# The two first wqkv loads of a one-core mixer kernel, issued from ScalarE's queue instead of SyncE's

## The chip, the cores and the metric

The kernel runs on one core of one Trainium2 chip. The metric is the device time of one execution in microseconds (us), the median of several executions. Engines are named as in the profile: PE (TensorE matmul), PEld (TensorE weight load), DVE (VectorE), ACT (ScalarE), POOL (GpSimd), SP (SyncE, which computes nothing and issues DMAs). An engine name with q behind it (SPq, PEq) is that engine's instruction sequencer.

## The reference

The input `x` has 2048 rows of 512. All tensors are fp32.

```python
xn = layernorm(x)
s  = A(xn, wqkv, wo)            # dilated sliding-window attention
g  = silu(B(xn, w1, b1, w2, b2))
out = x + s * g

def A(x, wqkv, wo):             # 32 heads of 16, window 8, dilation 2
    q, k, v = split(x @ wqkv)   # wqkv: 512 x 1536
    # each position attends to positions pos, pos-2, ..., pos-14
    return softmax(q k^T / 4, masked) v @ wo

def B(x, w1, b1, w2, b2):       # layernorm -> dense 1376 -> gelu -> dense 512
    return gelu(layernorm(x) @ w1 + b1) @ w2 + b2
```

## The kernel before

The 2048 positions are split into two classes by parity (dilation 2), and each class into 8 row tiles of 128. The 32 heads form 4 head blocks of 8; a pass over one head block makes q, k and v of 8 row tiles with PE (line 912) and then the window's logits and sums on DVE and POOL. The two dense layers of B run between these passes (lines 1192 and 1236), and the output projection is at lines 1104 and 1136. fp32 operands are split into a high and a low fp16 part and multiplied in three products; so weights and activations are scaled, cut and subtracted on ACT, DVE and POOL before PE can use them.

Every operation of the kernel is recorded in a plan with what it reads and writes. The table `ORDER` then says in which order the operations are written into the program: each engine runs its own in that order, and waits are put in where data or buffers need them. No engine passes over one of its instructions that still waits. A DMA is recorded as an operation of a queue `sp`, and is written as `nc.sync.dma_start`, so SP issues it. A DMA is also made to wait for the one that used its completion semaphore before it; there are eight such semaphores in turn.

What matters here is the start of the program. SP issues the loads; up to the ninth their order is

- **x0**, row tile 0 of x (256 KB, line 1283),
- **T7** and **T6**, the transposed row tiles 7 and 6 (256 KB each, line 1308),
- **x1**, row tile 1 (256 KB),
- **Q0**, first half of head block 0 of wqkv (384 KB, line 593, 128 partitions of 3072 bytes),
- **x2**, row tile 2 (256 KB),
- **Q2**, the second half of that block (384 KB, line 593),
- more tiles of x (256 KB each), then the next head block and the weights of B (line 1310).

Q0 and Q2 land in the two halves of a buffer `prod`. They are used twice. ACT squares each half and sums the squares (line 602, `scale_q`); PE adds the sums over partitions (line 518), DVE makes a scale of it (lines 529 to 547), and ACT and others cut the scaled weights into high and low parts (lines 632, 639, 558). And PE multiplies the raw fp32 halves with T7 and T6, whose mean has been taken off (line 724, `direct`: results `z` for T7 and `pl` for T6; the first two of the four steps over k read Q0, the other two Q2).

Before these stands, on PE, a row of matmuls on constants (line 1355), the means of T7 and T6 (lines 701 and 713), and the transposes of the normalised row tile 0 (line 808). That tile's path is: x0 lands, DVE takes its statistics (lines 672, 673, 753), POOL the root (757) and the normalisation (787), then PE transposes, ACT copies the result (812). For row tile 1 the normalisation is on ACT (783); its statistics are taken together with those of row tile 2, so it needs x2 too.

Of the kernel before, what the change touches and what calls it, by code (L numbers as in the profile page):

```python
# [13 lines left out]
ALU = mybir.AluOpType  # L14
# [4 lines left out]
P = 128  # L19
# [12 lines left out]
NFB = 7  # L32
LASTC = (0, 256, 512)
LASTPOOL = (0, 2, 4)
NX = 5

W1C = [0, 2048, 4096, 5120, KT * F]
# [30 lines left out]
MEANBY = ('dve', 'pe', 'pool', 'pool')  # L68
W2LATE = 6
SUBS = ()  # L70
ST_ENG = ('dve',) * 8
YLO = ('dve',) * 8
SECS = BATCHES
# [334 lines left out]
def tile_mixer(ctx, tc, a_x, a_xt, a_xo, a_wqkv, a_wo, b_w1, b_b1, b_w2, b_b2, out):  # L408
    nc = tc.nc
# [14 lines left out]
    def pe(n, cols, fn, r, w, fp32=1, **k):  # L424
        pl.add("pe", n * cols * 0.423e-3 * fp32, fn, r, w, **k)

    def dve(n, fn, r, w, f=1.0, port=True, c=0.065, **k):
        pl.add("dve", c + n * DVE1 * f, fn, r, w, port=port, **k)
# [4 lines left out]
    def pool(dur, fn, r, w, port=True, **k):  # L433
        pl.add("pool", dur, fn, r, w, port=port, **k)

    def dma(nbytes, fn, r, w, **k):
        pl.add("sp", 0.0, fn, r, w, nbytes=nbytes, **k)
# [52 lines left out]
    def f32v(t, k):  # L490

        names = " ".join("abcdefg"[:len(t.shape) - 1])
        return t.rearrange(f"p {names} -> p ({names})").bitcast(F32).rearrange(
            "p (k f) -> p k f", k=k)
# [67 lines left out]
    def split(hi, lo, src, s, r, w, eng="act", n=None, low="dve"):  # L562
# [8 lines left out]
        if low == "pool":  # L571
# [9 lines left out]
    stq = [lambda: xq0.t[:, 0:1536], lambda: U[1][:, 2048:3584],  # L581
           lambda: f32v(yT[2], 1)[:, 0, 0:1536], lambda: f32v(yT[3], 1)[:, 0, 0:1536]]
# [3 lines left out]
    def k0(hb):  # L586
        return dict(rate=400e3, tail=0.6, issue=0.45) if hb == 0 else dict(tail=3.5) if hb > 1 else {}


    def load_q(hb, kk=range(0, KT, 2)):  # L590
        pre = pl.users([x for x in stkey[hb] if x is not xq0])
        for k in kk:
            dma(P * 3072, lambda k=k: nc.sync.dma_start(stq[hb]()[:, k * 384:(k + 2) * 384],
                                                        a_wqkv[hb, :, k * 384:(k + 2) * 384]),
                [], [("stq", hb, k), ("stq", hb, k + 1)] + stkey[hb], after=pre, **k0(hb))

    def scale_q(hb):
# [88 lines left out]
    def parts(i):  # L686
        return ((0, 1), (1, KT)) if i in SUBS else ((0, KT),)

# [43 lines left out]
    def stats_act(i):  # L732
        q, (x, xkey) = cpos[i], xk[i]
        sm = R_s.new()
        o, dst = (i % 4) * P, yT[i // 4]
        junk = dst[:, 0, :, o:o + P].bitcast(BF16)
        act(512, lambda: nc.scalar.activation(x(), x(), AF.Identity, accum_out=sm.t[:, 0:1]), [xkey], [xkey, (sm, 0)], aps=2)
        act(1, lambda: nc.scalar.activation(mv0[:, q, 0:1], sm.t[:, 0:1], AF.Identity, scale=1.0 / D), [(sm, 0)], [("mv0", i)])
        act(1, lambda: nc.scalar.activation(sm.t[:, 1:2], sm.t[:, 0:1], AF.Identity, scale=-D ** -1.5), [(sm, 0)], [(sm, 1)])
        act(512, lambda: nc.scalar.activation(  # L740
            junk, x().rearrange("p (k t) -> p k t", k=KT), AF.Square, bias=sm.t[:, 1:2], scale=D ** -0.5,
            accum_out=mv0[:, q, 1:2]), [xkey, (sm, 1), ("mv0", i)], [("mv0", i), ("yh", 0, i)], aps=3)

    def ln0(g):
        q, n = cpos[g[0]], len(g)
        for i in g:
            if ST_ENG[i] == "act":
                stats_act(i)
# [377 lines left out]
    def wo_last():  # L1126
        rings = [R_ps, R_ps, R_ps, R_pl] + R_z
        end = PR_M * 10
        early, late = range(NHB - 1), [NHB - 1]
        rw = [("oT", hb, h) for hb in early for h in range(2)] + [("wo", k) for k in (0, 2)]  # L1130

        def mm(b, i, hbs, cols, start, stop):
            def go():
                for hb in hbs:
                    for n, (s, t) in enumerate(((0, 0), (0, 1), (1, 0))):
                        nc.tensor.matmul(b.t[:, cols], wo[:, t, hb, i % 4 * P:(i % 4 + 1) * P],  # L1136
                                         oT[:, hb, i // 4, s].rearrange("p t x -> p (t x)")[:, cols],
                                         start=(start and hb == 0 and n == 0), stop=(stop and hb == NHB - 1 and n == 2))
            return go

        parts = [(i, slice(0, D)) for i in range(NI - 1)] + [(NI - 1, slice(a, b)) for a, b in zip(LASTC, LASTC[1:])]
        banks = {}
        for n, (i, cols) in enumerate(parts[:NI]):
            b = banks[n] = rings[n].new()
            w = cols.stop - cols.start
            pe(9, w, mm(b, i, early, cols, True, False), rw + [("A", 7)] * (rings[n] is R_pl), [b], prio=end + 2 * n)
        for i in range(4):
            dma(P * 2048, lambda i=i: nc.sync.dma_start(gu[i], gd[1, i]),
                [("gd", 1, i), ("U0end",)], [("gu", i)], prio=end)
        xs = {}  # L1150
        for n, (i, cols) in enumerate(parts):
            w = cols.stop - cols.start
            if n < NI:
                if i < 7:
                    xb = R_f.new()
                    xs[i] = (lambda xb=xb: xb.t), xb
                else:
                    xs[i] = (lambda: U[0][:, NI * D:(NI + 1) * D]), ("gux",)
                dma(P * 2048, lambda x=xs[i][0], i=i: nc.sync.dma_start(x(), xo[1, i]),
                    [("oT", NHB - 2, 0), ("U0end",)], [xs[i][1]], prio=end + i)  # L1160
                b = banks[n]
                pe(3, w, mm(b, i, late, cols, False, True), [("oT", hb, i // 4) for hb in late], [b], prio=end + 2 * n + 1)
            else:
                b = R_ps.new()
                pe(12, w, mm(b, i, range(NHB), cols, True, True), rw + [("oT", hb, i // 4) for hb in late], [b],
                   prio=end + 2 * n + 1)
            x, xkey = xs[i]
            g = gu[i][:, cols]
            dve(w, lambda b=b, g=g, cols=cols: nc.vector.scalar_tensor_tensor(  # L1169
                g, b.t[:, cols], osc[:, 2:3], g, op0=ALU.mult, op1=ALU.mult),  # L1170
                [b, ("gu", i), ("osc",)], [("gw", n)], port=False, c=0.125)
            if n in LASTPOOL:
                pool(1.27, lambda x=x, g=g, cols=cols: nc.gpsimd.tensor_tensor(g, g, x()[:, cols], op=ALU.add),
                     [("gw", n), xkey], [("gw", n)])
            else:
                dve(w, lambda x=x, g=g, cols=cols: nc.vector.tensor_tensor(g, g, x()[:, cols], op=ALU.add),  # L1176
                    [("gw", n), xkey], [("gw", n)])
            dma(P * 4 * w, lambda g=g, i=i, cols=cols: nc.sync.dma_start(ov[1, i][:, cols], g),
                [("gw", n)], [("out", 1, n)], tail=0.7)
# [119 lines left out]
    s2a, s2b = f32v(yT[2], 4), f32v(yT[3], 4)  # L1299
    s2c = [R_f.new() for k in range(NX)]  # L1300

    def load(kind, i, last=()):
        if kind == "q":
            load_q(i // 4, [i % 4])
        elif kind == "x":
            load_x(i, 1)
        elif kind == "t":
            dma(P * 2048, lambda: nc.sync.dma_start(xt[i], a_xt[FP.index(i)]), [], [("xt", i)], rate=395e3, tail=0.6, issue=0.45)
        elif kind == "w":
            dma(P * 4 * (W1C[i + 1] - W1C[i]), lambda: nc.sync.dma_start(  # L1310
                s1[i](), b_w1[:, W1C[i]:W1C[i + 1]] if i < 3 else b_w1[:, W1C[3]:].rearrange("p (k e) -> p k e", k=KT)), [], s1k[i],
                rate=400e3, tail=0.8)
        elif kind == "s":
            dma(P * 8192, lambda: nc.sync.dma_start((s2a, s2b)[i], b_w2[:, 4 * i:4 * i + 4]), last,
                [("yT", 2 + i), ("s2", i)])
        elif kind == "b":
            dma(P * 428, lambda: nc.sync.dma_start(b1T, b_b1), [], [("b1T",)], rate=60e3)
        else:
            p0, w = (FL, D) if i == 4 else (0, D if i < 3 else P)
            dma((P - p0) * 4 * w, lambda: nc.sync.dma_start(s2c[i].t[p0:P, 0:w], b_w2[p0:P, 8 + i, 0:w]), last, [s2c[i]])  # L1320
# [32 lines left out]
    for n in range(WAKE):  # L1353
        b = R_z[0].new()
# [18 lines left out]
    with pl.fuse():  # L1373
# [14 lines left out]
                                           op1=ALU.max), [ssh], [ssh], port=False)  # L1388
# [4 lines left out]
    for m, (f0, f1) in enumerate(W1P):  # L1393
        n = min(f0 // 4, 2) if f0 < 10 else 3
# [32 lines left out]
    for m, k in enumerate(W2P):  # L1427
        n, K = (2, P) if k < 8 else (1, P)
# [32 lines left out]

    pl.prio = PR_U + 800
    load_q(2)
    prep_q(2)
    pl.prio = PR_U + 900
    load_q(3)
    prep_q(3)

# [16 lines left out]
    osc = sb.tile([P, 4], F32, name="osc")  # L1485
# [89 lines left out]
```

## Time and profile before

| | us |
|---|---|
| median of 3 executions (406.83, 406.97, 408.04) | 406.97 |
| the profiled execution | 407.78 |
| its span, first to last instruction | 406.0 |
| PE busy in it | 399.9 |
| DVE busy | 377.6 |
| ACT busy | 237.8 |
| POOL busy | 133.0 |

The profiled execution's own time is 1.78 us over its span. Busy time is summed over instructions and a busy PE need not be at its peak, so PE's 399.9 us say that it hardly ever stands idle, and not more. DMA queues: one queue (q1, issued by SP) carries all data, 47.82 MB.

### The profile page before, as it was taken

The numbers are of one execution on the slowest core, as the hardware profiler recorded it, in microseconds if no ns is written. First come the engines' busy times: TensorE is split into PE (matmuls) and PEld (weight loads), VectorE is DVE, ScalarE is ACT, GpSimd is POOL, SyncE is SP. The second block draws the span as 40 slices with busy tenths as digits, with TensorE's granted clock in tenths as the row PEclk, the third lists the DMA queues.
The fourth block names the chain that finished last, engine by engine and source line by source line (L and its number), as shares of the span: only waits on it lengthen the run. The fifth ranks groups of instructions, "written<-read, shape, count | busy, mean of one in ns | idle before, by whom it ended". The sixth has DMA issues, their size and how long they took to land.

```text
span 406.0 us, 5527 instructions
## 1 busy us (share of the span) xinstructions
PE 399.9 (99%) x2030; PEld 199.3 (49%) x2030; DVE 377.6 (93%) x382; ACT 237.8 (59%) x408; POOL 133.0 (33%) x139
## 2 busy tenths in 40 slices
PE   7999999999999999999999999999999999999996
PEld 5665544444444455445544554444455544444443
DVE  5998999999998999999999989999899889999966
ACT  2999889789689545775383243215252567345260
POOL 4713000072562534242524424242524204250012
PEclk9999999999999999999999999999999999999999
DMA  7948826240039260804571016231430755205566
GB/s 273 412 104 212 255 73 174 84 160 2 1 68 226 71 105 0 192 11 106 109 193 53 0 31 172 94 102 31 148 105 0 137 123 146 82 27 136 136 157 233
DMA packets 53827, 48.17 MB, mean 119 GB/s; under 512 B 38236, under 2 KB 38808, under 8 KB 53288
## 3 DMA queue, kind: packets, MB, share of 16 engines
q1 hardware_dynamic: 53800, 47.82, 43.7%
q8 instruction: 16, 0.26, 0.3%
q14 instruction: 11, 0.09, 0.1%
HBM read 24.27 MB, written 7.34 MB: 78 GB/s over the span
## 4 chain that ended last, share of the span: by engine, by line
PE 96%; DMA 2%; SPq 1%; DVE 1%; ACT 0%; issue 0%; DVEq 0%
PE ps L912 30%; PE ps L1192 26%; PE z L1236 26%; PE ps L1104 5%; PE z L1136 2%; PE ps L1136 2%; PE z L1224 2%; DMA prod<-in_A_wqkv_dram 2%; PE pl L912 1%; PE pl L1136 1%; PE pl L724 1%; PE z L808 0%; PE z L1227 0%; SPq L1283 0%; DVE U L1169 0%; DVE U L1176 0%
## 5 line engine op out<-in xcount | busy, mean ns | idle before, releaser
L912 PE MATMUL ps<-wq,yT 128*128 128x384 f16 (+1 forms) x708 | 129.5, 337 | 0.0
L1236 PE MATMUL z<-h,w 128*128 128x512 f16 x480 | 112.2, 379 | 0.0
L1192 PE MATMUL ps<-yT,w 128*128 128x512 f16 x480 | 108.9, 379 | 0.0
L912 PEld LDWEIGHTS <-yT 128*128 128x128 f16 x744 | 72.4, 98 | 58.4 <-issue 0.5
L1192 PEld LDWEIGHTS <-w 128*128 128x128 f16 x480 | 46.7, 98 | 55.7 <-issue 0.5
L978 DVE TENSOR_TENSOR prod<-U 128x2048 f32<-128x2048 f32 x32 | 73.2, 2288 | 0.9
L981 DVE TENSOR_REDUCE L<-prod 128x128 f32<-128x2048 f32 x32 | 73.0, 2282 | 0.4
L1236 PEld LDWEIGHTS <-w 128*128 128x128 f16 x480 | 46.7, 98 | 54.0
L1047 POOL TENSOR_TENSOR prod<-prod,prod 128x1024 f32<-128x1024 f32 x14 | 41.4, 2974 | 72.1 <-DVE prod L1036 72.1
L1036 DVE TENSOR_TENSOR prod<-pl,U 128x2048 f32<-128x2048 f32 x28 | 63.4, 2282 | 0.2
L930 ACT ACTIVATE U<-ps,cs 128x384 f32<-128x384 f32 x56 | 31.5, 576 | 48.0 <-PE ps L912 47.4
L1205 ACT ACTIVATE ps<-ps,b1T,hsc 128x512 f32<-128x512 f32 x40 | 29.7, 747 | 36.8 <-PE ps L1192 36.7
L1208 ACT ACTIVATE h<-ps,hsc 128x512 f16<-128x512 f32 x40 | 27.2, 683 | 17.8 <-PE z L1236 9.0
L1057 POOL COPY gate<-prod 1x1 f32<-1x1 f32 x21 | 5.0, 237 | 96.5 <-DVE prod L978 96.5
L1058 POOL TENSOR_TENSOR prod<-prod 128x1024 f32<-128x1024 f32 x14 | 32.9, 2349 | 0.0
L1210 DVE SCALAR_TENSOR_TENSOR h<-ps,hsc,h 128x512 f16<-128x512 f32 x40 | 29.7, 743 | 1.7 <-ACT h L1208 1.7
L1104 PE MATMUL ps<-oT,wo 128*128 128x512 f16 x96 | 22.0, 379 | 0.0
L1019 ACT ACTIVATE o<-prod,osc 128x1024 f16<-128x1024 f32 (+1 forms) x9 | 9.4, 1050 | 20.9 <-POOL prod L1058 10.5
L1205 ACT ACT_TABLE_LOAD x11 | 14.1, 1283 | 11.7 <-PE ps L1192 11.5
L1031 DVE TENSOR_TENSOR prod<-prod,prod 128x2048 f32<-128x2048 f32 x9 | 20.6, 2283 | 0.1
L1058 POOL TENSOR_TENSOR prod<-prod,prod 128x1024 f32<-128x1024 f32 x7 | 16.4, 2344 | 0.0
L992 POOL MEMSET L<- 1x56 f32 (+5 forms) x48 | 4.1, 185 | 37.5 <-DVE L L981 37.5
(194 smaller groups left out, 407.2 us busy)
## 6 DMA issues: line engine op xcount, KB each, us to landing
U<-U SPq DMA_DIRECT2D x16, 392.0 KB, 4.9
f<-in_A_x_dram SPq DMA_DIRECT2D x16, 256.0 KB, 3.0
f<-in_A_xo_dram SPq DMA_DIRECT2D x15, 256.0 KB, 3.8
gd<-f SPq DMA_DIRECT2D x12, 256.0 KB, 2.4
prod<-in_A_x_dram SPq DMA_DIRECT2D x8, 256.0 KB, 6.4
oT<-in_B_w_dram SPq DMA_DIRECT2D x2, 1024.0 KB, 7.8
yT<-in_B_w_dram SPq DMA_DIRECT2D x2, 1024.0 KB, 5.2
f<-gd SPq DMA_DIRECT2D x8, 256.0 KB, 3.0
```

Source lines behind the costliest of these rows:

```text
L912: nc.tensor.matmul(b.t[:, 0:wide], y[:, s, k, o:o + P], wq[hb][:, t, k], start=(n == 0), stop=(n == 11))
L930: act(384, lambda i=i, b=b: nc.scalar.activation(U3[:, i:i + 31:15, :], b.t[:, 0:384].rearrange("p (t e) -> p t e", t=3), AF.Identity, sca ...
L978: dve(2048, lambda p2=p2, g=g: nc.vector.tensor_tensor(p2(), q, slots(Ut, KH, 2 * g), op=ALU.mult), qk + [("kh", ub, 0), ("kh", ub, 1), (" ...
L981: dve(2048, lambda pr=pr, g=g: nc.vector.tensor_reduce(L3()[:, 2 * g:2 * g + 2], pr.t.rearrange("p (r f d) -> p r f d", r=2, d=DH), AX.X, ...
L1036: dve(2048, lambda: nc.vector.tensor_tensor(pr.t.rearrange("p (r f d) -> p r f d", r=2, d=DH), A3()[:, 2 * g:2 * g + 2].rearrange("p r (f ...
L1047: pool(2.4, lambda n=n: nc.gpsimd.tensor_tensor(acc.t[:, n:n + 1024], acc.t[:, n:n + 1024], p1.t[:, n:n + 1024], op=ALU.add), [acc, p1], [ ...
L1058: nc.gpsimd.tensor_tensor(x.t[:, 0:1024], x.t[:, 0:1024], y(), op=ALU.add)
L1104: nc.tensor.matmul(b.t, wo[:, t, hb, i % 4 * P:(i % 4 + 1) * P], oT[:, hb, i // 4, s], start=(hb == 0 and n == 0), stop=(hb == last and n ...
L1192: nc.tensor.matmul(b.t[0:M], w1[:, s, f * 512 + k * M:f * 512 + (k + 1) * M], yT[ch][:, t, k], start=(n == 0), stop=(n == 11))
L1205: act(512, lambda: nc.scalar.activation(b.t[0:M], b.t[0:M], AF.Gelu_apprx_tanh, bias=b1T[0:M, f:f + 1], scale=hsc[0:M, 1:2]), [b, ("b1T",) ...
L1210: dve(512, lambda: nc.vector.scalar_tensor_tensor(lo()[0:M], b.t[0:M], hsc[0:M, 2:3], hi()[0:M], op0=ALU.mult, op1=ALU.subtract), [b, hk], ...
L1236: nc.tensor.matmul(z.t, w2[:, w, f, blk[t]], hl[s], start=(f == 0 and n == 0), stop=False)
```

## The change

A constant `ACTQ = 1` is added, and `load_q` issues the loads of every head block below it, so those of head block 0 alone, with `nc.scalar.dma_start`. They then stand among ACT's instructions, and go through ACT's own DMA queue. The plan still records them as operations of `sp`, and `ORDER` is not touched. The constant `LASTPS` is `False`, so the second part of the diff writes the same instructions as before.

```diff
+LASTPS = False
...
+ACTQ = 1
...
     def load_q(hb, kk=range(0, KT, 2)):
         pre = pl.users([x for x in stkey[hb] if x is not xq0])
         for k in kk:
-            dma(P * 3072, lambda k=k: nc.sync.dma_start(stq[hb]()[:, k * 384:(k + 2) * 384],
-                                                        a_wqkv[hb, :, k * 384:(k + 2) * 384]),
+            dma(P * 3072, lambda k=k: (nc.scalar if hb < ACTQ else nc.sync).dma_start(
+                stq[hb]()[:, k * 384:(k + 2) * 384], a_wqkv[hb, :, k * 384:(k + 2) * 384]),
                 [], [("stq", hb, k), ("stq", hb, k + 1)] + stkey[hb], after=pre, **k0(hb))
```

On SP, at the start of the program, these are the loads before; `prod_99` is the buffer of Q0 and Q2, `prod_98` and `prod_100` hold row tiles of x, `U_92` holds T7 and T6 (and later the next head block).

```order
1 L1283 DMA prod_98<-in_A_x_dram 128x512
2 L1308 DMA U_92<-in_A_xt_dram 128x512 x2
3 L1283 DMA prod_98<-in_A_x_dram 128x512
4 L593 DMA prod_99<-in_A_wqkv_dram 128x768
5 L1283 DMA prod_98<-in_A_x_dram 128x512
6 L593 DMA prod_99<-in_A_wqkv_dram 128x768
7 L1283 DMA prod_100<-in_A_x_dram 128x512
8 L1283 DMA prod_98<-in_A_x_dram 128x512
```

And these are the same place after the change (lines have moved by 2 to 6):

```order
1 L1289 DMA prod_98<-in_A_x_dram 128x512
2 L1314 DMA U_92<-in_A_xt_dram 128x512 x2
3 L1289 DMA prod_98<-in_A_x_dram 128x512 x2
4 L1289 DMA prod_100<-in_A_x_dram 128x512
5 L1289 DMA prod_98<-in_A_x_dram 128x512
6 L1289 DMA prod_100<-in_A_x_dram 128x512
7 L595 DMA U_92<-in_A_wqkv_dram 128x768 x2
```

Q0 and Q2 are gone from SP's list; x2 now stands directly behind x1, and the others close up.

On ACT, the first instructions before are the load of its function table, the square of Q0, the copy of row tile 0's transpose, the square of Q2, and the normalisation of row tile 1.

```order
1 L602 ACT_TABLE_LOAD
2 L602 ACTIVATE wq_80,s_123<-prod_99 128x768
3 L812 CAST yT_87<-z_148 128x4x128
4 L602 ACTIVATE wq_80,s_123<-prod_99 128x768
5 L781 ACTIVATE rb_153<-pb_152,rb_153 128x1
6 L783 ACTIVATE prod_98<-prod_98,rb_153 128x512
```

After the change:

```order
1 L595 DMA prod_99<-in_A_wqkv_dram 128x768
2 L604 ACT_TABLE_LOAD
3 L604 ACTIVATE wq_80,s_123<-prod_99 128x768
4 L595 DMA prod_99<-in_A_wqkv_dram 128x768
5 L814 CAST yT_87<-z_148 128x4x128
6 L604 ACTIVATE wq_80,s_123<-prod_99 128x768
7 L783 ACTIVATE rb_153<-pb_152,rb_153 128x1
8 L785 ACTIVATE prod_98<-prod_98,rb_153 128x512
```

Q0 is now ACT's first instruction. Q2 stands behind the square of Q0, which waits for Q0 to land. PE, DVE and POOL have the same instructions in the same order as before.

## Rows read from the trace of the kernel before

**Rows 1.** The page: span, and busy time of each engine.

```profile
span 406.0 us, 5527 instructions
PE 399.9 (99%) x2030; PEld 199.3 (49%) x2030; DVE 377.6 (93%) x382; ACT 237.8 (59%) x408; POOL 133.0 (33%) x139
```

**Rows 2.** Busy time by stretch: window, length, engines' busy us, clock, DMA share, GB/s.

```profile
11.10:400.00 388.90, 388.90 (x1976) 191.90 (x1976) 368.57 (x363) 234.14 (x402) 125.75 (x126) 1.00 0.43 112
```

**Rows 3.** Waits of PE: for whom, us in total, times, longest.

```profile
PE z L808 <- POOL prod L787: 0.3, 1, 0.3
...
PE z L724 <- DMA prod<-in_A_wqkv_dram: 0.2, 1, 0.2
```

**Rows 4.** The chain that ended last, its beginning: start, length, what.

```profile
3.55 6.45 DMA prod<-in_A_wqkv_dram
...
10.02 0.94 ACT wq L602 x2
...
11.17 2.04 PE pl L724 x6
13.22 0.44 PE z L808 x4
```

**Rows 5.** Timeline: the path of x0 to PE (start, length, instruction, idle before).

```profile
0.73 0.40 SPq L1283 DMA_DIRECT2D prod<-in_A_x_dram  x1
...
3.49 0.69 DVE L672 BATCH_NORM_STATS2 bn<-prod 128x6 f32<-128x512 f32 x1 [2.36 <-DMA prod<-in_A_x_dram]
...
5.43 2.08 POOL L787 TENSOR_SCALAR prod<-prod,mv,rb 128x512 f32<-128x512 f32 x1
...
7.56 0.66 PE L808 MATMUL z<-first,prod 128*128 128x128 f32 x4 [0.34 <-POOL prod L787]
8.45 2.51 PE L724 MATMUL z<-prod,U 128*128 128x384 f32 x6 [0.23 <-DMA prod<-in_A_wqkv_dram]
```

**Rows 6.** Timeline: ACT and PE around the landings of Q0 and Q2.

```profile
8.33 0.84 ACT L602 ACTIVATE wq<-prod 128x768 bf16<-128x768 f32 x1 [6.33 <-DMA prod<-in_A_wqkv_dram]
...
10.04 0.91 PE L724 MATMUL z<-prod,U 128*128 128x384 f32 x2
...
11.04 2.18 PE L724 MATMUL pl<-prod,U 128*128 128x384 f32 x6
```

**Rows 7.** Timeline of SP: issues of loads.

```profile
2.60 0.43 SPq L593 DMA_DIRECT2D prod<-in_A_wqkv_dram  x1
...
4.50 1.06 SPq L1283 DMA_DIRECT2D prod<-in_A_x_dram  x1
...
8.33 0.33 SPq L1283 DMA_DIRECT2D prod<-in_A_x_dram  x1
8.99 0.33 SPq L1283 DMA_DIRECT2D prod<-in_A_x_dram  x1
...
10.67 0.33 SPq L1310 DMA_DIRECT2D h<-in_B_w_dram  x1
```

**Rows 8.** By stretch: window, length, PE busy, clock, DMA share, GB/s.

```profile
1.70:2.90 1.20, 1.20 (x8) 1.00 0.78 229
...
8.00:10.00 2.00, 1.75 (x6) 1.00 1.04 405
```

**Rows 9.** Timeline: T6 and x2 to their users, and PE's next transposes.

```profile
5.63 1.04 DVE L704 TENSOR_REDUCE f<-U 128x128 f32<-128x512 f32 x1 [1.04 <-DMA U<-in_A_xt_dram]
6.73 0.49 PE L713 MATMUL ps<-f,first 128*128 128x128 f32 x2 [0.25 <-DVE f L704]
...
9.00 0.69 DVE L672 BATCH_NORM_STATS2 bn<-prod 128x6 f32<-128x512 f32 x1 [0.34 <-DMA prod<-in_A_x_dram]
...
11.35 0.81 ACT L783 ACTIVATE prod<-prod,rb 128x512 f32<-128x512 f32 x1
...
13.05 0.60 PE L808 MATMUL z<-first,prod 128*128 128x128 f32 x4
```

**Rows 10.** Groups of PE, 3.0 to 4.6 us, then 5.6 to 6.5: mean ns.

```profile
L1355 PE MATMUL z<-first,fours 128*128 128x256 bf16 x9 | 2.1, 417 | 0.0
...
L1355 PE MATMUL z<-first,fours 128*128 128x256 bf16 x3 | 0.5, 272 | 0.0
```

More of the change, by code (lines that the diff above doesn't have):

```diff
@@ L1168, in wo_last @@
             g = gu[i][:, cols]
-            dve(w, lambda b=b, g=g, cols=cols: nc.vector.scalar_tensor_tensor(
-                g, b.t[:, cols], osc[:, 2:3], g, op0=ALU.mult, op1=ALU.mult),
+            m = (lambda g=g: g) if n in LASTPOOL or not LASTPS else (lambda b=b, cols=cols: b.t[:, cols])
+            dve(w, lambda b=b, g=g, m=m, cols=cols: nc.vector.scalar_tensor_tensor(
+                m(), b.t[:, cols], osc[:, 2:3], g, op0=ALU.mult, op1=ALU.mult),
                 [b, ("gu", i), ("osc",)], [("gw", n)], port=False, c=0.125)
@@ L1174, in wo_last @@
                      [("gw", n), xkey], [("gw", n)])
+            elif LASTPS:
+                dve(w, lambda x=x, g=g, m=m, cols=cols: nc.vector.tensor_tensor(g, m(), x()[:, cols], op=ALU.add),
+                    [b, ("gw", n), xkey], [("gw", n)], port=False)
             else:
```

## The prediction, on record before the changed kernel ran

> **What bounds the kernel now.** I read the page first: PE is busy 399.9 of 406.0 us [rows 1]. The table by stretches says where the rest is: from 11.1 to 400 us PE is busy in all of 388.9 us [rows 2]. So nothing that happens after 11 us can be shortened by an earlier load, and whatever moves PE's position at 11 us moves the end by as much, unless a helper engine that was just in time is then late. PE's waits are short and all lie at the start [rows 3]; there the timeline has to be read instruction by instruction.
>
> Three paths meet on PE there. The chain that ended last begins with the issue of Q2 at 3.55; Q2 lands at 10.0, ACT squares it until 10.96, and PE's `pl` matmuls follow [rows 4]. The second path is x0's: it lands at 3.49, goes through DVE and then 2.08 us of POOL, and PE transposes at 7.56, having waited 0.34 us for POOL [rows 5]. Third, the first matmuls on Q0 start at 8.45, with 0.23 us of idle before them put down to Q0 [rows 5]. ACT shows the same landings from its side: the square of Q0 starts at 8.33 after 6.33 us of idle, and the last two of PE's six `z` matmuls start at 10.04, when Q2 is there [rows 6].
>
> How long do loads take? SP's issues from the eighth load on wait for a completion semaphore each, so their starts tell landings: Q0 at 8.33, x2 at 8.99, Q2 at 10.02 by the square in the chain [rows 4], the next tile at 10.67 [rows 7]. They come in the order of issue, 0.65 us apart for 256 KB and 1.03 us for 384 KB, and the transfers then run at 405 GB/s [rows 8]. At the very start they do not: 229 GB/s and a DMA share of 0.78 between 1.7 and 2.9 us, while x0 moves [rows 8].
>
> **What the change does.** Two issues of 0.43 us leave SP [rows 7]; what follows there is issued up to 0.9 us earlier. SP is not the limit, since from 8 us the engines move 405 GB/s anyway, so I cost this at nothing; the cover is that stream. ACT gets the two issues. The first stands before its table load, and ACT is idle until 8.33 [rows 6], so it costs ACT nothing either. The second stands behind the square of Q0 and before the copy of row tile 0, which waits for PE's transposes; 0.43 us are free there as long as Q0 lands well before 8 us.
>
> What moves is the order of bytes. Q0 is issued at the start together with x0, and no longer fifth. Four terms follow.
>
> *Q0.* It no longer stands behind 1 MB of other loads. It should land about when x0 does, at some 4.3 us (below), so PE's wait for it goes.
>
> *x0.* It now shares the engines with Q0's 384 KB. Bounds: 0, if x0 is served first or Q0 only fills the 0.22 that x0 leaves idle; 1.03 us, if all of Q0 goes ahead (384 KB in rows 7 and 4). Equal shares while x0 moves give 0.65 us, alternate rows of 2 and 3 KB almost the whole 1.03. I take 0.8. POOL's path follows x0 without slack, since PE waited for it [rows 5], so the transposes move from 7.56 to 8.36.
>
> The Trainium skill, "DMA: Bandwidth & Descriptors", section "Queues, rings and completion order", says that each DMA engine serves its queues in turn, a packet at a time. No row before has two data queues, so none shows it; by it x0 loses 0.65 to 1.03 us, by the row with the idle share it may lose nothing, and the transposes would start at 8.2 to 8.6 or at 7.56.
>
> *T7, T6.* They move by up to 1.03 too. T6 would land at 6.66 instead of 5.63; DVE's 1.04 and PE's 0.49 on it [rows 9] end at about 8.26 on the way to the transposes at 8.36. Covered, with nothing to spare; the two matmuls at 6.73 stand before the transposes on PE, so a later T6 would push these.
>
> *Q2.* ACT issues it after Q0 has landed (4.3), at worst after the square of 0.94 us [rows 4]: 4.3 to 5.3. x0 took 2.76 us from issue to use [rows 5] with nothing ahead of it; 384 KB take 0.4 more, and shares with SP's stream up to 1.03: Q2 lands at 7.5 to 9.5. Before it was 10.0. So that wait goes as well. What it takes from the stream it takes from x1 and x2: x2 lands up to 1.03 after 8.99, or at no change if Q2 comes later. I take 0.8 here too, as most of Q2 should be ahead.
>
> **The sum.** First the path over x0. Without waits for Q0 and Q2, PE goes through in 0.44 us for four transposes and 2.04 for six matmuls (both lengths from the chain, where nothing waits [rows 4]): `pl` would start at 7.56 + 0.44 + 2.04 = 10.04 instead of 11.04 [rows 6]. That is 1.00 us to win, and 0.8 of it goes to x0's delay: -0.2. On the way ACT copies row tile 0 and squares Q2 (about 1.5 us behind the transposes' end of 9.0), done at 10.5, before PE gets to its sums at 10.84; covered. Then the path over x2: its statistics start at 9.00, ACT's normalisation of row tile 1 ends at 11.35 + 0.81 = 12.16, and PE needs it at 13.05 [rows 9]: 0.89 us of slack, now 0.8 used. PE's transposes there could start at 12.96, against 13.05: -0.09. The later of the two paths decides: **-0.1 us**. If both delays are 0 it is -0.9, if both are 1.03 it is +0.14. After that PE runs as before, for 389 us without idle, so this is the sum for the end. The profiled execution took 407.78, so 407.7 against itself; its span is 406.0, the median of the runs shown is 0.81 lower than its time, and on that median I forecast **406.9**. The measurement tells about 0.3% from no change, 1.2 us; the whole forecast lies inside.
>
> **The rivals.**
> - *x0 is not held up, Q0 fills idle engines.* For: the 0.78 share in x0's stretch [rows 8]. Against: 0.22 of 1.2 us is about a quarter of a microsecond, too little for 384 KB. It gives -0.9: 406.1. Still within 0.3%, since 1.00 us is all there is to win.
> - *Q2 queues up (slower).* Its issue now depends on Q0's landing. If loads of both queues are served in order of issue, Q2, issued at 4.3 to 5.3, stands behind all that SP has issued by then: x0, T7, T6, x1, x2, two more tiles, and an eighth as soon as x0 has landed. Before, Q2 had x0, T7, T6, x1 and x2 ahead of it, and Q0 in both cases. So two or three tiles more, at 0.65 us each: it lands 1.3 to 1.95 us after 10.02, or 0.65 if SP's issues get stuck. `pl` follows 1.02 us behind it (10.02 to 11.04), so the end moves by +0.65 to +1.95: 407.6 to 408.9. From a landing at 11.24 on it is slower by over 0.3%. For it: landings before are strictly in order, and issues do get stuck, the eighth on SP took 1.06 us instead of 0.43 [rows 7]. Against: that was one queue, and the row with ACT's queue doesn't exist yet.
> - *The clock rises later.* The 256-column matmuls take 417 ns at first and 272 from about 5.7 us [rows 10]: the lower level (1.2 GHz) and then the upper (2.4), after PE has been busy since 1.19 us. If T7 is late by more than the slack that PE has on it (unknown: PE does not wait for it now), a gap of some tenths falls into that stretch. If the rise came only after the `z` matmuls, 0.44 + 2.04 us of work would take twice as long: +2.5 at most, 409.4.
>
> The Trainium skill, "DMA: Bandwidth & Descriptors", section "Issuing engines are not separate DMA queues", says that issuing from several engines saves only the time to issue. By it the change would win nothing from more bandwidth, which is how I summed; it says nothing on order, which is where the terms are.
>
> **How the numbers follow.** Forecast (shared engines, near -0.1) 0.56; x0 not held up 0.21; Q2 queued 0.17; later clock 0.06. The first two are within 0.3% but for scatter of the runs (408.04 among three), which I allow 0.03 on the fast side. Of Q2 queued about three quarters lies over the limit, of the clock a half, and 0.02 for the unforeseen: slower 0.18. Same 0.79. The likeliest case alone runs from 406.3 to 407.2; the range goes from just above the fast rival to the middle of the Q2 case: 406.2 to 408.4.
>
> **What the profile after will show.** A second data queue; ACT's square of Q0 at 4 to 5 us, not 8.33; DVE's first statistics at 4.1 to 4.5, not 3.49; PE's first transposes near 8.4 with POOL as the releaser; no wait of PE for Q0 or Q2; the chain beginning with x0, not Q2; `pl` at about 10.9; and 389 us of PE without idle behind that. I am wrong if Q2's square starts after 10.2, if x0 is not delayed, or if PE, arriving earlier, finds DVE, POOL or ACT late after 13 us, so that the start gains and the end doesn't.

## The result, and the profile after

The changed kernel is slower: 409.24 us in the median of 7 executions (408.87 to 411.48), against 407.14 for the kernel before (7 executions, 406.83 to 408.84). The ratio is 1.0048, with a 95% interval of 1.0033 to 1.0064. That is 2.1 us more, outside the range forecast. The profiled execution took 408.89 us with a span of 407.1, which is 1.1 us over the one before [rows 1].

The page of the changed kernel shows the same work, and a second data queue, q10 (in the queue lines: packets, MB, share of 16 engines' span). L724 is now L726, and L808 is L810.

```profile
span 407.1 us, 5528 instructions
PE 399.3 (98%) x2030; PEld 198.5 (49%) x2030; DVE 377.8 (93%) x382; ACT 237.6 (58%) x408; POOL 133.0 (33%) x139
...
q1 hardware_dynamic: 53512, 47.03, 42.8%
q10 hardware_dynamic: 288, 0.79, 0.6%
```

Behind the start nothing has changed. The stretch of [rows 2], by the same view of the changed kernel (length, busy time of PE, PEld, DVE, ACT, POOL, clock, DMA share, GB/s), leaves PE 0.05 us of idle in 388.9:

```profile
11.10:400.00 388.90, 388.85 (x1975) 191.88 (x1975) 368.24 (x362) 234.83 (x404) 126.03 (x126) 1.00 0.42 111
```

So the loss lies ahead of 11 us. The waits of PE there, which were 0.3 and 0.2 [rows 3], are now these (for whom, us in total, times, longest):

```profile
PE z L810 <- POOL prod L789: 1.2, 1, 1.2
...
PE ps L703 <- DMA U<-in_A_xt_dram: 1.2, 1, 1.2
PE ps L715 <- DVE f L706: 0.2, 1, 0.2
```

The wait for row tile 0's normalisation on POOL has grown from 0.3 to 1.2 us, and a new wait of 1.2 us has come, for T7. The chain that ended last (start, length, what) no longer begins with SP's issue of Q2, but it still runs through Q2:

```profile
0.73 4.36 DMA prod<-in_A_wqkv_dram
...
5.12 6.01 DMA prod<-in_A_wqkv_dram
...
11.16 0.37 ACT wq L604
...
12.31 2.04 PE pl L726 x6
14.35 0.44 PE z L810 x4
```

Q0 lands at 5.1 instead of 8.3, and that starts ACT's issue of Q2; Q2 then takes 6.01 us and lands at 11.16, where it landed at 10.02 [rows 4]. The timeline shows both paths (start, length, instruction, idle time before it and what ended that); ACT's come first, then those of x0 through DVE, POOL and PE:

```profile
0.73 0.40 ACTq L595 DMA_DIRECT2D prod<-in_A_wqkv_dram  x1
...
5.12 0.84 ACT L604 ACTIVATE wq<-prod 128x768 bf16<-128x768 f32 x1 [2.67 <-DMA prod<-in_A_wqkv_dram]
5.12 0.33 ACTq L595 DMA_DIRECT2D prod<-in_A_wqkv_dram  x1
...
11.16 0.84 ACT L604 ACTIVATE wq<-prod 128x768 bf16<-128x768 f32 x1 [0.53 <-DMA prod<-in_A_wqkv_dram]
...
5.29 0.69 DVE L674 BATCH_NORM_STATS2 bn<-prod 128x6 f32<-128x512 f32 x1 [4.16 <-DMA prod<-in_A_x_dram]
...
7.23 2.07 POOL L789 TENSOR_SCALAR prod<-prod,mv,rb 128x512 f32<-128x512 f32 x1
...
9.35 0.66 PE L810 MATMUL z<-first,prod 128*128 128x128 f32 x4 [1.23 <-POOL prod L789]
9.85 2.25 PE L726 MATMUL z<-prod,U 128*128 128x384 f32 x6
...
12.17 2.18 PE L726 MATMUL pl<-prod,U 128*128 128x384 f32 x6
```

x0 reaches DVE at 5.29 instead of 3.49, 1.80 us later. POOL and PE follow by as much, and the transposes start at 9.35 instead of 7.56 [rows 5]. From there PE needs 2.82 us to `pl`, where it needed 3.48 before: the wait for Q0 is gone and that for Q2 has become short. So 1.79 us of delay at the transposes is 1.13 us at `pl`: 12.17 against 11.04 [rows 6].

The two profiled executions differ by the 1.1 us that `pl` moved, the medians by 2.1. The profiled execution before lay 0.64 us over its median, the one after 0.35 under its own.

### The profile page after: what moved, and what is told of

Its sections match the earlier page's. It is cut to its first block, busy times and chain, and to the rows that moved or that the text cites. A ratio compares the mean times of both kernels' runs of the same rounds, so it can differ in the third digit from the quotient of the medians.

```text
span 407.1 us, 5528 instructions
## 1 busy us (share of the span) xinstructions
PE 399.3 (98%) x2030; PEld 198.5 (49%) x2030; DVE 377.8 (93%) x382; ACT 237.6 (58%) x408; POOL 133.0 (33%) x139
## 4 chain that ended last, share of the span: by engine, by line
PE 96%; DMA 3%; DVE 1%; issue 0%; ACT 0%; DVEq 0%
PE ps L914 30%; PE ps L1198 26%; PE z L1242 25%; PE ps L1106 5%; DMA prod<-in_A_wqkv_dram 3%; PE z L1138 2%; PE ps L1138 2%; PE z L1230 2%; PE pl L914 1%; PE pl L1138 1%; PE pl L726 1%; PE z L810 0%; PE z L1233 0%; DVE U L1172 0%; DVE U L1182 0%; PE z L726 0%
```

## The experiments

Two things were late, and the first question was what each costs alone. The theory after the result: two delays add up. **Start**: Q0, sent at the same moment as x0, holds x0 up by more than Q0's own transfer time. **Queue**: a load on ACT's queue that is issued late waits until the loads that SP had issued are through. The rivals: only the second counts and x0's delay is swallowed by the waits that fall away; or the gap ahead of T7 delays the rise of PE's clock. Each kernel was timed against the kernel before on the same chip; medians, and the ratio with its interval, are from all those executions.

**The kernel before, once more.** No edit.

> The kernel before, unchanged. Every theory expects the same time as before within 0.2%. It gives a second profile of before, with the spans and clocks of several executions, since the first profiled execution was 0.7 us over the median: if x0 lands at 3.5 us and pl starts at 11.0 us again, the start of the program is not what differs between executions.

It took 407.61, the kernel before beside it 407.73: ratio 0.9996 (0.9987 to 1.0005). So differences of 0.1% can be told here. Its profiled execution had x0 at 3.33 and `pl` at 11.00, as [rows 5] and [rows 6], and in addition one wait of 0.5 us much later; it took 408.43, over its own median.

**Q0 alone on ACT's queue, Q2 back on SP's.**

```diff
-(nc.scalar if hb < ACTQ else nc.sync)
+(nc.scalar if hb < ACTQ and k == 0 else nc.sync)
```

> Only Q0 is issued by ACT; Q2 goes back to its place on SP, so its issue waits for nothing. Theory A (x0 held up by Q0 is the loss): x0 at 5.3 us, PE's first transposes at 9.35, pl near 11.9 instead of 12.2; 0.3 us under the changed kernel, some 0.8 to 1.7 us over before. Theory B (Q2 issued behind the square of Q0 is the loss): Q2 lands near 10 as before, and the time is back at before within 0.3 us.

It took 408.79 against 407.73: ratio 1.0024 (1.0015 to 1.0033), 1.06 us. x0 is as late as in the changed kernel, and PE waits for POOL, not for Q2:

```profile
5.32 0.69 DVE L674 BATCH_NORM_STATS2 bn<-prod 128x6 f32<-128x512 f32 x1 [4.18 <-DMA prod<-in_A_x_dram]
...
9.38 0.66 PE L810 MATMUL z<-first,prod 128*128 128x128 f32 x4 [1.24 <-POOL prod L789]
...
11.87 1.54 PE L726 MATMUL pl<-prod,U 128*128 128x384 f32 x4
```

So the start alone costs 0.83 us at `pl` and about 1 us in the median. A second measurement of the same kernel on another chip gave more:

> Only Q0 on ACT, once more, beside the three others of this set: 1.0024 of before within 0.1%, x0 at 5.3 us, Q2 by 10, pl at 11.9.

It took 409.02 against 407.37, ratio 1.0043 (1.0027 to 1.0059), with x0 at 5.61 and `pl` at 12.15. The start is then worth 1.06 to 1.65 us of the 2.1. This kernel and the changed one were not timed beside each other on one chip, so the difference between them, which is Q2's part, is known only roughly.

**Q0 ahead of x0 in one queue.** The kernel before, without the change; in `ORDER`, Q0's load (operation 1) moves ahead of x0's (operation 4).

```diff
-    4, 110, 109, 111, 112, 113, 114, 115, 108, 37, 116, 6, 117, 38, 40, 0, 19, 118, 119, 8, 1, 120, 121, 122,
+    1, 4, 110, 109, 111, 112, 113, 114, 115, 108, 37, 116, 6, 117, 38, 40, 0, 19, 118, 119, 8, 120, 121, 122,
```

> One queue: SP issues Q0 ahead of x0, all else in the order of before. The bytes ahead of x0 are those of the changed kernel, without a second queue. If order of bytes is all, x0 lands 1.0 us later than before, at 4.5 us, transposes at 8.6, pl near 11.1 and the time within 0.3 us of before. If x0 lands at 5.3 as with two queues, +0.8 us or more.

This is the case that I had priced as the worst for x0: all of Q0 goes first. x0 arrives at 4.53, 1.04 us later than before, near the 1.03 of the prediction (the four profiles with x0 first in one queue have it at 3.25 to 3.49, so a hundredth means nothing here). With two queues it was 5.29. The bytes moved up to the moment at which DVE has x0 say what the difference is. These are the DMA queues of three kernels, from 0 to that moment (packets, MB, share of 16 engines); of the kernel before, up to 3.49:

```profile
q1 hardware_dynamic: 268, 0.50, 43.7%
```

of Q0 first in one queue, up to 4.53:

```profile
q1 hardware_dynamic: 401, 0.87, 58.6%
```

and of the changed kernel, up to 5.29:

```profile
q1 hardware_dynamic: 391, 0.73, 36.8%
q10 hardware_dynamic: 144, 0.39, 25.2%
```

Q0 is 0.39 MB. Without it SP's loads had moved 0.50, 0.48 and 0.73 MB when x0 was complete. In one queue x0 waits for Q0 and for nothing else. With two queues another 0.23 MB of what SP issued behind x0 (T7, T6) went through before x0's last part; at the 383 GB/s that the engines moved there from 3.2 to 5.2 us, that is 0.6 us. Together with 1.04 it makes 1.6 of the 1.80. Why x0's last part falls behind T7 is not shown; one reading is that some of the 16 engines are still busy with Q0's packets while others are already past x0.

In time the kernel is not better: 408.75 against 407.73, ratio 1.0039 (1.002 to 1.0059). In its profile `pl` starts at 11.46, not at the 11.1 expected, and a later wait of 0.4 us for DVE comes on top. About 0.4 us of that (my estimate) is not x0's: POOL is done at 8.53, but PE is behind, since T7's matmuls take 2.08 us here and 1.16 in the changed kernel; so the transposes start at 8.68 and are slow themselves. Its executions are also the most scattered of all (408.08 to 411.69), see the clock below. So the step of 0.8 us between one queue and two is shown in x0's landing, not in the medians.

**Q2 issued by ACT ahead of the square of Q0**, so that it doesn't wait for Q0's landing.

```diff
-    49, 123, 124, 125, 3, 32, 26, 2, 128, 126, 127, 20, 7, 27, 9, 53, 21, 54, 50, 28, 10, 5, 29, 51, 56, 55, 52,
+    49, 123, 124, 125, 3, 2, 32, 26, 128, 126, 127, 20, 7, 27, 9, 53, 21, 54, 50, 28, 10, 5, 29, 51, 56, 55, 52,
```

> Both loads on ACT, Q2 issued right behind Q0 and ahead of the square. Theory A: Q2 is there by 7 us, and the time still stands 0.8 us or more over before, since x0 is as late as in the changed kernel or later, and T6 is later too. Theory B: the late Q2 is gone, so the time falls to before or 1 us below it.

It took 410.03 against 407.73: ratio 1.0054 (1.0041 to 1.0067). ACT no longer waits for Q2, but now 768 KB stand beside x0, T7 and T6: PE idles 2.14 us for T7, whose matmuls start at 6.90 and take 2.07 us, and `pl` starts at 12.23; a later wait of 0.6 us for DVE comes on top. The wait is moved from Q2 to T7, not removed.

**The changed kernel again.** No edit.

> The changed kernel once more, on the same chip as the three others of this set, for a second profile and more times: 1.0048 of before within 0.15%. In its first profile the start was 1.1 us late, while the medians differ by 2.0: if pl starts well after 12.2 us here, the landing of Q2 differs between executions; if it starts at 12.2 and the matmuls before are at the lower clock, it is the clock.

It took 409.68 against 407.37: ratio 1.0062 (1.0041 to 1.0082). In this profile Q2 was issued at 5.44 and landed at 11.94, 6.5 us later, and PE itself waited for it:

```profile
PE z L726 <- DMA prod<-in_A_wqkv_dram: 0.7, 1, 0.7
```

`pl` started at 12.95, 0.78 us later than in the first profile, and the execution was 409.67 against 408.89, 0.78 us longer. So the changed kernel has two bounds close together, x0 and Q2, and Q2 can be the later one. The issues say why Q2 landed later here. In both profiles SP issues its eighth load at the moment at which x0 is ready for DVE, and ACT issues Q2 when Q0 has landed. Here x0 came first (5.25), and one more load of 256 KB stood ahead of Q2:

```profile
5.24 0.33 SPq L1289 DMA_DIRECT2D prod<-in_A_x_dram  x1
...
5.44 0.33 ACTq L595 DMA_DIRECT2D prod<-in_A_wqkv_dram  x1
```

In the first profile Q2 was issued at 5.12, ahead of that load:

```profile
5.29 0.33 SPq L1289 DMA_DIRECT2D prod<-in_A_x_dram  x1
```

**Q2 alone on ACT's queue, Q0 back on SP's.**

```diff
-(nc.scalar if hb < ACTQ else nc.sync)
+(nc.scalar if hb < ACTQ and k == 2 else nc.sync)
```

> Q0 stays on SP in its old place; only Q2 is on ACT, behind the square of Q0. x0, T7 and T6 are undisturbed; Q0 lands at 8.3 or up to 0.3 us earlier, Q2 is issued then. Theory Q (a late load on ACT stands behind all that SP has issued): Q2 lands 5.5 to 6.5 us later, at 13.5 to 15, pl 1 us behind, the time 3.5 to 5 us over before. Equal shares: Q2 lands 3 to 3.5 us after its issue, at 11.4, the time 1.4 us over before. If Q2's place does not matter to the end: as before.

This takes x0 out of the question (it is at DVE at 3.46) and enlarges the other: 414.5 against 407.37, ratio 1.0177 (1.0163 to 1.0192). PE's wait for it:

```profile
PE z L726 <- DMA prod<-in_A_wqkv_dram: 5.1, 1, 5.1
```

The timeline of ACT, and then of SP:

```profile
7.99 0.38 ACTq L595 DMA_DIRECT2D prod<-in_A_wqkv_dram  x1
...
14.75 0.84 ACT L604 ACTIVATE wq<-prod 128x768 bf16<-128x768 f32 x1 [5.35 <-DMA prod<-in_A_wqkv_dram]
...
3.08 2.27 SPq L1289 DMA_DIRECT2D prod<-in_A_x_dram  x4
5.39 1.96 SPq L595 DMA_DIRECT2D U<-in_A_wqkv_dram  x2
```

ACT issues Q2 at 7.99, as soon as Q0 has landed. SP has by then issued eleven loads, 3.28 MB. From 8.4 to 11.2 us the queues show one line, without q10, and the second line gives what has moved from 0 to 11.2:

```profile
q1 hardware_dynamic: 511, 1.14, 104.7%
...
q1 hardware_dynamic: 1530, 3.15, 82.9%
```

and from 11.2 to 13.9 both:

```profile
q1 hardware_dynamic: 321, 0.70, 68.0%
q10 hardware_dynamic: 142, 0.39, 37.2%
```

For 3.2 us after its issue Q2 moves nothing, until all but 0.13 MB of the eleven loads are through; then 142 of its 144 packets pass in 2.7 us beside SP's. So ACT's queue isn't slow to start (in the changed kernel Q0, issued at 0.73, moves 26 packets between 1.5 and 2.3 us), and SP's isn't simply served first, for SP had issued more loads by 11.2 us and these share with Q2. The changed kernel shows the same on a smaller scale: Q2 is issued at 5.12, and from 5.5 to 7.5 us only q1 moves:

```profile
q1 hardware_dynamic: 412, 0.76, 99.4%
```

Q2's first packet follows at 7.81, when SP's queue has moved 1.68 of the 1.84 MB issued ahead of Q2; in the second profile it is 8.65 and 1.90 of 2.10 MB. The queue theory holds: here a load on ACT's queue stood behind nearly all that SP had issued before it, and then shared with what SP issued later. The Trainium skill, "DMA: Bandwidth & Descriptors", section "Queues, rings and completion order", says that an engine takes a packet from each of its queues in turn; for two loads issued together the trace of the changed kernel is near that in the end (up to 4 us 133 packets of q10 and 144 of q1), for one that is issued later it is not, and the measurement decides. Whether Q2's packets were at the engines' disposal during those 3.2 us, the trace doesn't show.

PE's idle time of 5.1 us has a price of its own. This is the granted clock (the number behind the brackets) during it and after it, in PE's view by stretch:

```profile
12.00:14.70 2.70, 0.00 (x0) 0.54 1.09 423
16.00:18.00 2.00, 2.00 (x6) 0.50 1.02 394
18.00:20.00 2.00, 2.00 (x7) 0.74 1.05 426
```

The clock has fallen to the lower of its two levels, 1.2 of 2.4 GHz, and PE computes at it until about 19 us. `pl` starts 5.3 us late (16.31) and takes 3.53 us for the six matmuls that take 2.18 in [rows 6], and the median is 7.1 us over that of the kernel before.

**Six more constant matmuls ahead of T7**, so that PE isn't idle there: the changed kernel with this edit.

```diff
-        pl.add("pe", 0.2, lambda b=b: nc.tensor.matmul(b.t[:, 0:2 * P], fours, mean1.bitcast(BF16), start=True,
-                                                       stop=True), [], [b], prio=1e9)
+        pl.add("pe", 0.2, lambda b=b, n=n: [nc.tensor.matmul(b.t[:, 0:2 * P], fours, mean1.bitcast(BF16), start=True,
+                                                             stop=True) for m in range(1 + (10 <= n < 16))], [], [b],
+               prio=1e9)
```

> The changed kernel with six more matmuls on constants ahead of the mean of T7 (22 instead of 16), which fill PE's 1.2 us of idle until T7 lands and compute nothing that is used. If the clock rises later in many executions of the changed kernel because of that gap, the time falls by 0.5 to 1 us against the changed kernel. If the gap is harmless for the clock, the time is that of the changed kernel within 0.2 us, or 0.2 longer where the fill runs past T7.

PE has no idle time before T7 any more. It took 409.34 against 407.37, ratio 1.0053 (1.004 to 1.0066), where the changed kernel beside it had 1.0062. With the gap of 1.2 to 1.45 us filled the loss stays, so the gap ahead of T7 is not its main cause. In this profile Q2 was again behind SP's eighth load (5.08 and 5.27); it landed at 11.59, PE waited 0.5 us for it, and `pl` started at 12.60.

**Q0 issued a little later.** An activation on one constant element is put ahead of Q0's issue on ACT. It was meant to hold the load back behind the function table's 1.28 us. It didn't: the issue went out at 0.79 while the table load ran from 0.73 on. But 0.06 us seems to be enough to matter. Three kernels have this edit: with Q0 alone on ACT, with both loads in the changed order, and with Q2 ahead of the square.

```diff
+                if hb < ACTQ and k == 0:
+                    nc.scalar.activation(ssq[0:1, 3:4], nc.const_aps.tensor(0.0, [1, 1]), AF.Square)
```

Q0 alone:

> Only Q0 on ACT, and behind the one-element activation, which moves ACT's issue from 0.73 to 0.79 us, 0.06 us behind SP's issue of x0. If the loads of both queues are taken up one after the other in the order of their issue, x0's first packets come first and x0 lands at 4.8 us instead of 5.3; pl at 11.3 to 11.4, 0.5 us less than with Q0 on ACT alone, at 1.001 of before. If the 0.06 us do not matter and the queues only share, the time is that of Q0 on ACT alone.

408.89 against 407.37, ratio 1.003 (1.0017 to 1.0043), where the same without the 0.06 us, on the same chip, gave 1.0043 (1.0027 to 1.0059). These overlap, and the 1.001 expected did not come; the profiles differ: x0 is at DVE at 4.91 instead of 5.61, and `pl` starts at 11.46 instead of 12.15. The timeline shows ACT's table load and issue, then SP's issue of x0:

```profile
0.73 1.28 ACT L597 ACT_TABLE_LOAD   x1 [0.73 <-PEq L1542]
0.79 0.38 ACTq L598 DMA_DIRECT2D prod<-in_A_wqkv_dram  x1
...
0.74 0.41 SPq L1293 DMA_DIRECT2D prod<-in_A_x_dram  x1
```

Between 1.5 and 2.3 us one queue alone moves, SP's:

```profile
q1 hardware_dynamic: 33, 0.07, 53.5%
```

In the kernel without the delay (Q0 issued at 0.73, x0 at 0.74) it is in the same stretch the other queue, alone:

```profile
q10 hardware_dynamic: 23, 0.07, 42.8%
```

Both loads, in the changed order:

> As the run with both behind the table load, but Q2 is left behind the square of Q0, as in the changed kernel. x0 is undisturbed, so what is lost is Q2's alone. Theory Q (a load issued on ACT late stands behind all that SP has issued by then): Q0 lands at 6 to 7.5, Q2 is issued then and lands 4 to 6 us later, at 11 to 13; pl 1 us behind that, 1 to 3 us over before. If both queues are served at equal shares, Q2 lands within 3.5 us, by 10.5, and the time is within 0.5 us of before.

408.73 against 407.37, ratio 1.003 (1.0019 to 1.0041), about six tenths of the loss of the changed kernel beside it. x0 comes at 4.79, Q2 is issued at 5.22 and lands at 10.89, `pl` starts at 11.90. Both loads, with Q2 ahead of the square:

> Both loads on ACT, one behind the other, but behind a one-element activation on a constant (an addition to the program) that pulls the table load ahead: Q0 is issued at about 2.2 us instead of 0.7, Q2 at 2.6, both ahead of the square. Theory A (the harm is that Q0's bytes go together with x0's, T7's and T6's): x0 is back at 3.4 us, T7 and T6 within 0.5 of before, Q0 and Q2 land at 7 to 9.5, pl starts at 10.2 to 11.0: time from before down to 0.8 us below it. Theory C (a second queue of itself costs, wherever its loads stand): 1 us or more over before.

409.5 against 407.37, ratio 1.0052 (1.004 to 1.0064). Both loads went out together at 0.79, so this is the Q2-ahead kernel once more: T7 late (6.23), T6 later (PE waits 0.80 us for DVE's reduction of it), and from 8.5 to 13 us the granted clock is 0.62 on average; the six `z` matmuls take 3.16 us instead of 2.10, and `pl` starts at 12.94.

**SP alone, Q2 ahead of x2.** The kernel before with operations 2 (Q2) and 3 (x2) exchanged in `ORDER`, to see whether any gain can be had at the start.

```diff
-    49, 123, 124, 125, 3, 32, 26, 2, 128, 126, 127, 20, 7, 27, 9, 53, 21, 54, 50, 28, 10, 5, 29, 51, 56, 55, 52,
+    49, 123, 124, 125, 2, 32, 26, 3, 128, 126, 127, 20, 7, 27, 9, 53, 21, 54, 50, 28, 10, 5, 29, 51, 56, 55, 52,
```

> One queue as before, but Q2 changes places with x2, so it is issued right behind Q0. Q2 lands at 9.35 instead of 10.0, x2 at 10.0 instead of 9.0. The wait for Q2 shrinks by 0.65 us, and the normalisation of row tile 1, which needs x2, is 1.0 us later with 0.9 us of slack: between 0.3 us below before and 0.2 over, 1.000. If it is faster by more, there was room for a better order of loads without a second queue.

`pl` starts at 9.96, 1.08 us earlier than [rows 6], and yet the kernel is 0.8 us slower, more than the 0.2 expected at most: 408.18 against 407.37, ratio 1.0018 (1.0009 to 1.0028). PE's timeline has two new waits behind `pl`:

```profile
9.96 2.18 PE L724 MATMUL pl<-prod,U 128*128 128x384 f32 x6
12.57 0.65 PE L808 MATMUL z<-first,prod 128*128 128x128 f32 x4 [0.43 <-ACT prod L783]
...
16.89 0.66 PE L808 MATMUL z<-first,prod 128*128 128x128 f32 x4 [0.63 <-DVE prod L790]
```

Row tile 1 and a later one are not ready when PE arrives. Row tile 1 is also a little later itself, as x2 is (ACT's normalisation starts at 11.71 instead of 11.35). The 0.89 us of slack that the prediction read on x2's path [rows 9] is about all that there is: who takes 1.08 us out of the start meets the next late helper.

Across the profiles one number puts these together: from the start of `pl` to the end of the span every kernel needs the same 394.9 to 395.2 us, unless a later wait or a slower clock comes on top.

| profiled execution | x0 at DVE | `pl` starts | span | span less `pl` | on top, behind `pl` |
|---|---|---|---|---|---|
| before | 3.49 | 11.04 | 406.0 | 395.0 | |
| before, once more | 3.33 | 11.00 | 406.6 | 395.6 | a wait of 0.5 |
| Q0 alone on ACT | 5.32 | 11.87 | 406.8 | 394.9 | |
| Q0 alone, again | 5.61 | 12.15 | 407.3 | 395.2 | |
| Q0 alone, 0.06 later | 4.91 | 11.46 | 407.2 | 395.7 | a wait of 0.4 |
| changed | 5.29 | 12.17 | 407.1 | 394.9 | |
| changed, more fill | 5.09 | 12.60 | 407.5 | 394.9 | |
| changed, again | 5.25 | 12.95 | 407.9 | 395.0 | |
| Q0 0.06 later, Q2 at the square | 4.79 | 11.90 | 407.0 | 395.1 | |
| Q2 ahead of the square | 5.20 | 12.23 | 408.0 | 395.8 | a wait of 0.6 |
| the same, 0.06 later | 4.74 | 12.94 | 407.9 | 395.0 | |
| Q2 alone on ACT | 3.46 | 16.31 | 412.6 | 396.3 | the lower clock until 19 us |
| Q0 first in SP's queue | 4.53 | 11.46 | 406.9 | 395.4 | a wait of 0.4 |
| SP alone, Q2 ahead of x2 | 3.25 | 9.96 | 406.3 | 396.3 | waits of 0.4 and 0.6 |

## Why the prediction was wrong

The forecast was 406.9, and the case that came was the rival "Q2 queues up", together with a larger delay of x0 than any that I had allowed. Two terms of the sum failed: x0's, which was too small, and Q2's, whose mechanism was another. By its steps:

- **What bounds the kernel: right.** PE has no idle time after `pl`, and a shift of `pl` is a shift of the end (table above).
- **Q0: right for PE, but late.** The wait of `z` for Q0 is gone, as said. It landed at 5.12 and 5.44, not at 4.3, and as its landing lets ACT issue Q2, that issue came at the late end of the 4.3 to 5.3 that I gave it, or behind it.
- **x0: mis-sized, and the bound was wrong.** I took 0.8 and at most 1.03; it was 1.80 and 1.76 in the two profiles. The upper bound rested on "if all of Q0 goes ahead", which costs 1.04 in one queue. With two queues, bytes that SP issued behind x0 also pass before x0 is complete. Worked into the sum of the prediction, the path over x0 would give 1.8 - 1.0 = +0.8 at `pl` instead of -0.2; Q0 alone on ACT's queue measured +0.83 and +1.11 there.
- **T7 and T6: covered, but only because x0 was later still.** T6 came 0.91 us later (6.54 against 5.63), within the 1.03. T7 came later than that: PE needed it at 4.55 before without waiting, and got it at 5.94. PE's new idle of 1.18 us for T7 lies ahead of the transposes, which stand behind POOL until 9.35.
- **Q2: the mechanism was wrong.** I let it share with SP's stream at a price of at most 1.03 us and land at 7.5 to 9.5; it landed at 11.16 and 11.94. From its issue at 5.12 to its first packet at 7.81 it shared nothing: 2.7 us in which SP's earlier loads moved. The rival had 11.3 to 12.0, from SP's loads ahead of it in order of issue, and the run with Q2 alone on ACT shows just this. So does the spread: with seven loads of SP ahead of it Q2 landed at 11.16 (and 10.89 with Q0 0.06 later), with eight at 11.94 (and 11.59 with more fill). I gave it 0.17 because the trace of before had one queue only; that is no reason against it, and the row that spoke for it, strict order of landings, was the only one there. What Q2 adds beside x0's delay is less sure, since Q0 alone varies too: 0.0 to 1.1 us at `pl` (12.17 and 12.95, against 11.87 and 12.15), and 0.5 to 1.2 us in the medians (2.10 and 2.31, less the 1.06 to 1.65 of Q0 alone), from different chips.
- **x2 and ACT's own time: no loss, but by another way.** No wait of PE goes to row tile 1's normalisation, and the issues cost ACT no time. The normalisation is 0.96 us later all the same (12.31 against 11.35), since on ACT it stands behind the square of the late Q2; PE is later by more.
- **The clock: hardly in the profiles of the changed kernel, but not out of the question.** Filling the gap changed nothing that is clear of noise, and in both profiles T7's eight matmuls took 1.16 us. In five other profiles (Q0 first on SP, Q0 alone again, Q0 alone 0.06 later, Q0 0.06 later with Q2 at the square, Q2 ahead of the square) they took 2.07 to 2.08 us, which speaks for the lower of the two levels (1.2 GHz). The clock column of the views reads 1.00 there, but only because the trace has no record of the clock so early; its first record, at full speed, starts at 9.0 to 9.8 us in these five, and at 4.1 to 5.7 us in all others. Where Q0 alone was on ACT, that lay beside POOL's path. In Q0 first on SP and in Q2 ahead of the square PE reached the transposes 0.15 and 0.58 us after POOL had done its part, and the slow matmuls cost about 0.4 and 0.5 us at `pl` (my estimates).
- **A few long executions: open.** One execution in seven of the changed kernel and one in six in its second measurement took 411.48 and 412.22 at a mean granted clock of 0.992; two of twelve with Q0 first on SP (411.58 and 411.69) and one of nine of Q0 alone, again, (411.52) had the same clock. None of 79 of the kernel before took over 408.9. That is near the 2.5 us that the prediction gave as the most for a late clock; no such execution was profiled.
- **Two slips in reading.** The prediction says that SP's eighth load waits for a semaphore and that its issue took 1.06 us [rows 7]. By the order of loads it is the ninth. No term of the sum hangs on it.

Also open is why the medians differ by 2.1 us when `pl` differs by 1.1 and 1.9. The two profiled executions of the kernel before were 0.6 and 0.8 us over its medians (0.5 of it a later wait in the second), so its usual execution may have an earlier `pl` than the profiles show. None of that kind was profiled.

## What to carry to other kernels

In these runs a load that was moved to another engine's queue did not get bandwidth of its own. So price such a load with all that the other queue has issued before it, and price what it is issued together with by more than its own bytes. A DMA issue in a compute engine's stream also inherits that engine's waits: here Q2's issue had to wait for Q0's landing, 1.6 us after SP had issued it before. And a gain at the start is worth no more than the slack of the next helper, so read that slack first.

## What the hardware showed that I had not expected

- The order of two issues 0.06 us apart decided which load's packets went first: x0 was ready at 4.91 with SP's issue ahead by 0.05 us, and at 5.61 with ACT's ahead by 0.01 us. Over all profiles it was ready at 4.74 to 4.91 where ACT's issue was 0.05 to 0.06 us behind SP's (three), and at 5.09 to 5.61 where it was not behind (six).
- ACT's DMA issue was not held by a table load and an activation ahead of it in the same stream (issue at 0.79, table load from 0.73 to 2.01, activation at 2.02), while an activation that waited for data did hold it (Q2's issue at 5.12, with the square of Q0).
- A 384 KB load took 5.7 to 6.8 us from issue to use when SP had loads outstanding (5.22 to 10.89, 5.12 to 11.16, 7.99 to 14.75), against 2.76 for x0, 256 KB, with nothing ahead of it [rows 5] and 4.4 for Q0 beside x0.
- Two queues together moved no more than one: 1.12 MB by 5.29 us in the changed kernel, 1.14 MB by the same time on SP's queue alone with Q2 ahead of x2.
